# Attention and a gated feed-forward layer on one core: one load moves up the queue, three visits move by part of a step

## The chip, the core and the metric

The kernel runs on one core of a Trainium2 chip. A core has TensorE (PE in the rows: matmuls, with weight loads beside them as PEld), VectorE (DVE), ScalarE (ACT), GpSimd (POOL) and SyncE (SP), which here only issues DMAs. They run side by side and wait for each other through semaphores. SBUF is the working memory, PSUM the memory that TensorE writes; DMAs move data between device memory and SBUF. The metric is the device time of one launch in microseconds (us).

## The reference

Eight batches of attention with eight heads of 64, 576 positions, a window of 128 keys and a linear bias, and behind it a feed-forward layer over all 4608 rows: 512 to 2048, an activation, 2048 to 512.

```python
scores = scale * np.matmul(q, k.transpose(0, 1, 3, 2))
mask = (rel >= 0) & (rel < window)
scores = np.where(mask, scores + bias[None], -1000000000.0)
scores = scores - np.max(scores, axis=-1, keepdims=True)
attn = np.exp(scores)
attn = attn / (np.sum(attn, axis=-1, keepdims=True) + 1e-09)
x = np.matmul(attn, v)            # heads side by side: 4608 rows of 512
h = x @ w_in
sp = np.where(h > 20.0, h, np.log1p(np.exp(np.minimum(h, 20.0))))
g = h * np.tanh(sp)
out = g @ w_out
```

## The kernel before

**The work.** The feed-forward layer runs in nine blocks: block c holds the first 512 rows of batch c (c from 0 to 7), and the ninth the last 64 rows of all batches, which were put aside in `xs`. A block has two layers. The first layer makes `h` (names `h`) in 8 pieces from x and the weights `si`; the activation turns it into `g`. The second layer takes 32 steps: each is 6 matmuls of 128x512 into one of two sums `po0`, `po1`, from the weights `so` and from a high and a low part of g, `gg`. ScalarE makes the high part by a copy, GpSimd the low part by a subtraction. After step 15 both sums are copied out as `ob`, and step 16 starts the next sums in the same PSUM banks. Every float32 product is made of three matmuls in a rounded form.

Attention of batch c+1 is laid between the matmuls of block c, in four pairs of heads. The first two batches are written out by hand in one list of names, `FIRST_STEPS` (line 28): there TensorE, VectorE, ScalarE, GpSimd and SyncE keep the list's order. From block 1 on, attention of batch c+1 (c from 1 to 6, six blocks) is placed by a table of numbers, and there only TensorE and SyncE keep the program's order; a scheduler orders the rest.

**The corners.** The last 64 queries of a pair of heads are laid out in the corners of a 128x128 square, so that one matmul scores two heads. For the second batch (batch 1) all four squares come by one load, `load_corners(1)`, into the tile `z1` (rows: `z`, 256 KB). That tile takes the one buffer of tag `pta`, which held the values of the last pair of batch 0 (`v0_3`); the matmuls `lV3`, which write `pt_3l`, read those last. `lC3` copies that pair's last small result and sends it to `xs` by SyncE. Before the change the load of the corners is issued behind the last piece of block 0's first layer (`Q7`): there the last weights (`wo7`, two halves), two loads of values (`v1_0`, `v1_1`) and then the corners go out on SyncE's queue. The first user of z1 is `lbS0`, the last-query scores of batch 1's first pair, in the middle of the first steps of block 0's second layer. Behind it in TensorE's order stand the scores `bS0` and `bS1` and then the next steps of the second layer.

While block 0 runs, the weights are still being turned into their rounded forms (`cE`, `cW`, `cU`, `cL` in the list, on ScalarE, VectorE, ScalarE and GpSimd; `wo`, `to`, `so` in the rows).

**The visits.** In blocks 1 to 6 the steps of the second layer have the keys 0 to 31, and the making of `gg` for step pair m the key 2m - 4.1. Attention is put in by the same kind of key, through the four numbers of `VISITS`. Visit k is where pair k's weights meet the values: `rest_values`, `values`, `keep`, `split_x`. The scores of pair p+2 stand just ahead of visit p (their own number is 0.001 less), and the softmax of that pair follows at fractions of the way to the next visit: biases and row minima on VectorE (they write the tile `pz`), exponentials on ScalarE, the scaling on GpSimd, a transposition in squares on VectorE, and the way out to device memory by SyncE (`d<-pz`; a first group of 384 KB, a second of 320 and 96 KB). Between `pz` in SBUF and the values stands a way back in: `pta<-d` and `ptb<-d`, issued behind the visit before. SyncE issues per visit: four `pta` and two `ptb` loads, the next pair of q and k (`qk`), the small result (`xs<-xo`), at one visit a load of values (`v`), then the three `d<-pz`.

`pz` has two buffers. So the first bias of pair 3 (ahead of visit 1) waits until the first `d<-pz` of pair 2 has left its buffer. The exponentials of pair 3 stand on ScalarE ahead of the two copies `ob` that step 16 waits for.

```python
        VISITS = (5.0, 13.3, 21.6, 29.9)
        def when(x):
            k = min(max(int(x // 1), 0), 2)
            return VISITS[k] + (VISITS[k + 1] - VISITS[k]) * (x - k)
```

With these numbers the scores of pair 2 get the key 4.99, ahead of step 5, and the values of pair 0 get 5.0 and a little more, behind step 5: step 5 stands between them. The other visits have all their parts between the same two steps.

Of the kernel before, what the change touches and what calls it, by code (L numbers as in the profile page):

```python
# [80 lines left out]
def attention_mish_mlp(  # L81
# [83 lines left out]
    def load(dst, src):  # L165
        sp.dma_start(out=dst, in_=src)

    def load_w(kind, j):

        n = 256 if kind == "i" else DM  # L170
        if kind == "i":
            src = w_in[:, j * 256 : (j + 1) * 256].rearrange("(c p) f -> p c f", p=P)
        else:
            src = w_out[j * 256 : (j + 1) * 256, :].rearrange("(c p) f -> p c f", p=P)
        if (kind, j) == last_w:

            halves = [
                xp.tile([P, 1024], U32, tag=f"x{NCC - 2 + a}", name=f"w{kind}{j}_{a}")
                for a in range(2)
            ]  # L180
        else:
            t = big(f"w{kind}{j}", U32)
            halves = [t[:, :1024], t[:, 1024:]]
        raw_w[(kind, j)] = halves
        for a, t in enumerate(halves):
            part = src[:, a * (512 // n) : (a + 1) * (512 // n), :]
            if bits:
                load(t.rearrange("p (c n) -> p c n", n=2 * n), part.bitcast(U32))
            else:
                load(t[:, :512].bitcast(F32).rearrange("p (c n) -> p c n", n=n), part)  # L190
# [77 lines left out]
    def parts_of(t):  # L268

        qk = t[:, : 2 * S].rearrange("p (a s) -> p a s", a=2)  # L270
        return lambda h, n0, n: qk[h, 0, n0 : n0 + n], lambda h, n0, n: qk[h, 1, n0 : n0 + n]
# [35 lines left out]
    def load_pair(b, p):  # L307
        t = at.tile([P, 2 * S], F32, tag="qk", name=f"qk{b}_{p}")
        load(t, qk_[b, p][:, : 2 * S])
        qkv[(b, p)] = parts_of(t)  # L310

    def load_v(b, p):

        pl, tag = (at, "pta") if (b, p) == (0, NP - 1) else (xp, f"x{p}")
        t = pl.tile([P, 2, 4, P], F32, tag=tag, name=f"v{b}_{p}", bufs=1)
        load(t, v[b, p])
        qkv[("v", b, p)] = ((t[:, 0], t[:, 1]), t[:64, 1, 3])
# [3 lines left out]
    def load_corners(b):  # L321

        t = corners[b] = at.tile([P, 2, 4, P], F32, tag="pta", name=f"z{b}", bufs=1)
        load(t[:, 0], qk_[b, :, :, 2 * S :].rearrange("a p n -> p a n"))
# [652 lines left out]

    def attention(b):

        VISITS = (5.0, 13.3, 21.6, 29.9)  # L980

        def when(x):
            k = min(max(int(x // 1), 0), 2)
            return VISITS[k] + (VISITS[k + 1] - VISITS[k]) * (x - k)

        def next_pair(p):
            nxt = (b, p + 2) if p + 2 < NP else (b + 1, p + 2 - NP)
            if nxt[0] < B:
                load_pair(*nxt)

        ahead, steps = {}, []
        for p in range(NP):
            if p > 1:
                steps += pair_steps(b, p) + [(p - 1.993, lambda p=p: next_pair(p))]
                continue
            before, beside, behind, in_out, ends = pair_steps(b, p)

            ahead[4 + 2 * p] = (before + [lambda p=p: next_pair(p)], beside, behind)
            if p:
                steps.append((0.005, in_out))  # L1000
            else:
                ahead[5] = ([], [], [in_out])
            steps += ends
        steps = [(when(x), f) for x, f in steps]

        steps += [(d, lambda p=p: load_v(b, p)) for p, d in enumerate((-0.5, -0.4, 6.5, 17.5))]
        return ahead, sorted(steps, key=lambda s: s[0])
# [152 lines left out]

    loads = {f"bS{2 * p + 1}": lambda p=p: load_pair(*((1, p + 2) if p < 2 else (2, p - 2))) for p in range(NP)}
    loads.update({f"bL{p}": lambda p=p: load_v(1, p + 2) for p in range(2)})
    loads.update({f"L{p + 2}": lambda p=p: load_pair(1, p) for p in range(2)})

    def add_conversions(ms):
        for m in ms:
            tag = f"po{m % 2}" if m < 6 else "wo"[m % 2]
            works = convert(*conv[m], tag, m in BY_ACT, dve if m == len(conv) - 1 else pool)
            steps.update(zip((f"cE{m}", f"cW{m}", f"cU{m}", f"cL{m}"), works))

    add_conversions(range(len(conv) - 2))
    for name in FIRST_STEPS.split():
        steps[name]()
        if name in loads:
            loads[name]()
        if name == f"Q{NJ - 1}":
            load_w(*last_w)
            add_conversions(range(len(conv) - 2, len(conv)))
            for p in range(2):
                load_v(1, p)  # L1180
            load_corners(1)
    dve.fixed = act.fixed = pool.fixed = False

    for c in range(1, B + 1):
        ahead, steps_beside = attention(c + 1) if c + 1 < B else ({}, [])
        for j in range(NJ):
            before, beside, behind = ahead.get(j, ([], [], []))
# [115 lines left out]
```

## Time and profile before

| | us |
|---|---|
| median of three runs | 951.16 |
| lowest and highest | 950.44, 953.33 |
| the profiled execution | 953.0 |
| its span, first to last instruction | 951.2 |
| TensorE busy in it | 931.4 |

The span is the time from the first to the last instruction of one profiled execution; launch and end lie around it. TensorE is busy in 98% of it, so what can be won is what TensorE waits for, and what it does more slowly than it does the same thing elsewhere. The timeline merges instructions of one kind that follow each other: a row gives start, length, engine, what is written and read, and how many; in square brackets stand the idle time before it and who ended it. Rows of matmuls overlap their successors by a little, since the ends of matmuls are modelled: the distance of two starts is the time that a group takes.

### The profile page before, as it was taken

What the parts mean: (1) busy time and instruction counts of PE and PEld (TensorE: products, weight loads), DVE (VectorE), ACT (ScalarE), POOL (GpSimd) and SP (SyncE); (2) the same over time, 40 slices, a digit from 0 to 9 for tenths busy, and PEclk for the clock granted to TensorE, in tenths of its full rate; (3) what the DMA queues carried; (4) which work ended last, traced back from release to release, by engine and by line L of the source; (5) the groups of instructions that cost most, each with busy time, mean ns of one, the idle gap of its engine ahead of it and who ended that gap; (6) DMA issues with size and microseconds to landing.
All of it is one profiled execution on the core that took longest, in us unless ns stands there. A gap on an engine that the chain in (4) does not pass through costs nothing.

```text
span 951.2 us, 17253 instructions
## 1 busy us (share of the span) xinstructions
PE 931.4 (98%) x6650; PEld 759.8 (80%) x6650; DVE 284.6 (30%) x1119; ACT 434.5 (46%) x1075; POOL 332.0 (35%) x300
## 2 busy tenths in 40 slices
PE   8997999999999999999999999999999999999998
PEld 6785888888888788887888788887888888888886
DVE  5996861333122510423033411341043300100000
ACT  6996752654254613744256424552374422322221
POOL 4585752135122531244123512244124411241042
PEclk9998999999999999999999999999999999999999
DMA  9963120337215540556024720545044520000001
GB/s 345 393 254 119 66 88 24 98 125 233 62 42 158 156 141 23 154 157 183 24 77 131 224 86 26 173 125 171 24 127 137 164 63 1 23 22 23 1 20 25
DMA packets 89745, 106.63 MB, mean 112 GB/s; under 512 B 22720, under 2 KB 69824, under 8 KB 89664
## 3 DMA queue, kind: packets, MB, share of 16 engines
q1 hardware_dynamic: 89664, 105.54, 34.7%
q8 instruction: 52, 0.85, 0.4%
q14 instruction: 29, 0.24, 0.1%
HBM read 75.37 MB, written 30.15 MB: 111 GB/s over the span
## 4 chain that ended last, share of the span: by engine, by line
PE 89%; ACT 5%; DMA 3%; DVE 1%; issue 1%; POOL 1%; SPq 0%; DVEq 0%; ACTq 0%; POOLq 0%
PE h L69 40%; PE po L69 38%; PE s L69 3%; PE o L69 3%; ACT pz L69 3%; DMA d<-pz 1%; PE w L69 1%; PE po0s L69 1%; PE os L69 1%; DMA v<-in_v_dram 1%; DMA z<-in_qk_dram 1%; DVE pz L69 1%; SPq L69 0%; ACT x L69 0%; POOL pz L69 0%
## 5 line engine op out<-in xcount | busy, mean ns | idle before, releaser
L69 PE MATMUL po<-so,gg 128*128 128x512 f32 x1728 | 407.7, 393 | 5.1 <-ACT ob L69 5.1
L69 PE MATMUL h<-x,si 128*128 128x512 f32 x1728 | 398.2, 390 | 0.0
L69 PEld LDWEIGHTS po<-so,gg 128*128 128x128 f32 x1728 | 321.2, 188 | 77.6 <-ACT ob L69 7.6
L69 PEld LDWEIGHTS h<-x,si 128*128 128x128 f32 x1728 | 323.0, 188 | 70.3 <-issue 3.3
L69 POOL TENSOR_TENSOR gg<-g,gg 128x512 fp32r<-128x512 f32 x144 | 185.2, 1288 | 412.1 <-ACT gg L69 411.8
L69 ACT ACTIVATE gg<-g 128x512 fp32r<-128x512 f32 x144 | 90.7, 630 | 177.6 <-PE po L69 175.3
L69 ACT ACTIVATE g<-h 128x1024 f32<-128x1024 f32 x72 | 73.9, 1027 | 193.5 <-PE h L69 193.4
L69 POOL TENSOR_TENSOR pz<-pz,sm 128x256 f32<-128x256 f32 (+4 forms) x96 | 97.2, 1030 | 168.1 <-DVE sm L69 141.2
L69 ACT ACTIVATE pz<-pz,mx 128x192 f32<-128x192 f32 (+1 forms) x280 | 120.2, 431 | 19.8 <-DVE mx L69 19.2
L69 DVE CUSTOM_DVE_ANT_0 pz<-s,nb 128x192 f32<-128x192 f32 (+1 forms) x160 | 46.9, 328 | 107.6 <-PE s L69 84.5
L69 ACT ACT_TABLE_LOAD x39 | 50.0, 1283 | 13.9 <-DVE mx L69 13.4
L69 DVE STREAM_TRANSPOSE pz<-pz 128x768 f32<-128x768 f32 (+2 forms) x72 | 49.2, 709 | 17.8 <-POOL pz L69 16.8
L69 DVE CUSTOM_DVE_ANT_0 pz<-os,nb 128x192 f32<-128x192 f32 x24 | 8.5, 355 | 151.5 <-PE ws L69 151.5
L69 ACT ACTIVATION_READ_ACCUMULATOR pz<-pz,mx 128x1 f32 x280 | 52.3, 187 | 0.0
L69 DVE COPY ob<-po 128x512 f32<-128x512 f32 x10 | 6.9, 692 | 137.4 <-PE po L69 137.4
L69 DVE COPY xo<-w 128x64 f32<-128x64 f32 x24 | 5.4, 224 | 116.1 <-PE w L69 115.7
L69 ACT ACTIVATE x<-o 128x256 fp32r<-128x256 f32 (+1 forms) x32 | 12.8, 401 | 46.6 <-PE w L69 46.1
L69 PEld LDWEIGHTS o<-pta,v 64*64 64x64 f32 (+1 forms) x768 | 27.7, 136 | 8.1 <-issue 6.4
L69 PE MATMUL o<-pta,v 64*64 64x64 f32 (+1 forms) x768 | 32.8, 226 | 0.0
L69 ACT ACTIVATE ob<-po 128x512 f32<-128x512 f32 x26 | 14.8, 593 | 34.1 <-PE po L69 34.1
L69 DVE DVE_READ_ACCUMULATOR2_ANT mx<- 128x1 f32 (+1 forms) x360 | 29.0, 81 | 0.0
L69 PE MATMUL s<-qk 64*64 64x192 f32 (+1 forms) x560 | 28.0, 326 | 0.0
(188 smaller groups left out, 579.1 us busy)
## 6 DMA issues: line engine op xcount, KB each, us to landing
v<-in_v_dram SPq DMA_DIRECT2D x32, 512.0 KB, 4.7
qk<-in_qk_dram SPq DMA_DIRECT2D x28, 576.0 KB, 4.6
d<-pz SPq DMA_DIRECT2D x24, 384.0 KB, 2.8
pta<-d SPq DMA_DIRECT2D x72, 128.0 KB, 2.8
wi<-in_moe_w_in_dram SPq DMA_DIRECT2D x16, 512.0 KB, 11.0
wo<-in_moe_w_out_dram SPq DMA_DIRECT2D x16, 512.0 KB, 10.2
out_dram<-ob SPq DMA_DIRECT2D x32, 256.0 KB, 2.0
d<-pz SPq DMA_DIRECT2D x24, 320.0 KB, 4.0
```

Of the source, the lines that this page charges most:

```text
L69: ins = method(*args, **kwargs)
```

## The change

The load of batch 1's corners is taken from behind `Q7` and put behind `lC3`, the copy of batch 0's last small result. `VISITS` becomes (5.5, 13.5, 21.5, 29.9).

```diff
-        VISITS = (5.0, 13.3, 21.6, 29.9)
+        VISITS = (5.5, 13.5, 21.5, 29.9)
...
     loads.update({f"bL{p}": lambda p=p: load_v(1, p + 2) for p in range(2)})
+    loads["lC3"] = lambda: load_corners(1)
     loads.update({f"L{p + 2}": lambda p=p: load_pair(1, p) for p in range(2)})
...
             for p in range(2):
                 load_v(1, p)
-            load_corners(1)
```

No instruction is added or removed. SyncE's queue at the end of block 0's first layer, before the change (`xs_95<-xo0_3l` is the last small result, `z1` the corners, `wo7` the last weights, `v1` values of batch 1):

```order
L69 DMA qk1_1_677<-in_qk_dram 128x1152
L69 DMA xs_95<-xo0_3l_734 128x64
L69 DMA wo7_0_1049<-in_moe_w_out_dram 128x1024
L69 DMA wo7_1_1050<-in_moe_w_out_dram 128x1024
L69 DMA v1_0_1054<-in_v_dram 128x1024
L69 DMA v1_1_1056<-in_v_dram 128x1024
L69 DMA z1_1058<-in_qk_dram 128x4x128
```

There the corners are the last of the seven. The same place on SyncE after the change:

```order
L69 DMA qk1_1_677<-in_qk_dram 128x1152
L69 DMA xs_95<-xo0_3l_734 128x64
L69 DMA z1_737<-in_qk_dram 128x4x128
L69 DMA wo7_0_1051<-in_moe_w_out_dram 128x1024
L69 DMA wo7_1_1052<-in_moe_w_out_dram 128x1024
L69 DMA v1_0_1056<-in_v_dram 128x1024
L69 DMA v1_1_1058<-in_v_dram 128x1024
```

The corners now stand ahead of four loads that they stood behind; all else on this queue keeps its place, here and in the rest of the program.

TensorE at visit 0 of block 1, before the change (`po1_0_1<-so2` is step 5, `s2_2` the scores of pair 2, `o2_0` and `w2_0` the first of the values of pair 0):

```order
L69 MATMUL po1_0_0_2218<-so2_181,gg1_0_2_2215 128x512 x6
L69 MATMUL s2_2_0_2256<-qk2_2_1997 64x192 x8
L69 MATMUL s2_2_1_2268<-qk2_2_1997 64x128 x4
L69 MATMUL s2_2_1_2268<-qk2_2_1997 64x192 x6
L69 MATMUL po1_0_1_2225<-so2_181,gg1_0_2_2215 128x512 x6
L69 MATMUL o2_0_2288<-pta2_0_2077,v2_0_2211 64x64
```

Step 5 stands between scores and values. The same place on TensorE after the change:

```order
L69 MATMUL po1_0_0_2218<-so2_181,gg1_0_2_2215 128x512 x6
L69 MATMUL po1_0_1_2225<-so2_181,gg1_0_2_2215 128x512 x6
L69 MATMUL s2_2_0_2262<-qk2_2_1997 64x192 x8
L69 MATMUL s2_2_1_2274<-qk2_2_1997 64x128 x4
L69 MATMUL s2_2_1_2274<-qk2_2_1997 64x192 x6
L69 MATMUL o2_0_2288<-pta2_0_2077,v2_0_2211 64x64
```

Step 5 moved from between the scores and the values to ahead of both. The same six times, in blocks 1 to 6; TensorE's order is otherwise unchanged, also at the other three visits.

VectorE behind the biases of pair 2 in block 1, before the change (`sm` are the sums of the softmax, `pz2_2_0` and `pz2_2_1` the two groups of pair 2, `xo2_0` and `x2_0` results of pair 0):

```order
L69 RECIPROCAL sm2_2_0_2266<-sm2_2_0_2266 128x4
L69 RECIPROCAL sm2_2_1_2280<-sm2_2_1_2280 128x5
L69 STREAM_TRANSPOSE pz2_2_0_2267<-pz2_2_0_2267 128x768
L69 COPY xo2_0_2330<-w2_0_2289 128x64
L69 TENSOR_TENSOR x2_0_2333<-o2_0_2288,x2_0_2333 128x256
L69 TENSOR_TENSOR x2_0_2333<-w2_0_2289,x2_0_2333 128x2x128
L69 STREAM_TRANSPOSE pz2_2_1_2281<-pz2_2_1_2281 128x640
L69 STREAM_TRANSPOSE pz2_2_1_2281<-pz2_2_1_2281 128x2x96
```

The first transposition stands third. The same place on VectorE after the change:

```order
L69 RECIPROCAL sm2_2_0_2272<-sm2_2_0_2272 128x4
L69 COPY xo2_0_2330<-w2_0_2289 128x64
L69 TENSOR_TENSOR x2_0_2333<-o2_0_2288,x2_0_2333 128x256
L69 RECIPROCAL sm2_2_1_2286<-sm2_2_1_2286 128x5
L69 TENSOR_TENSOR x2_0_2333<-w2_0_2289,x2_0_2333 128x2x128
L69 STREAM_TRANSPOSE pz2_2_0_2273<-pz2_2_0_2273 128x768
L69 STREAM_TRANSPOSE pz2_2_1_2287<-pz2_2_1_2287 128x640
L69 STREAM_TRANSPOSE pz2_2_1_2287<-pz2_2_1_2287 128x2x96
```

The copy and the two subtractions for pair 0 now stand ahead of the first transposition. On ScalarE the copy `gg` for steps 10 and 11 moved from between pair 2's exponentials to ahead of them, and one copy of pair 0's result to ahead of the second group's sums; on GpSimd the low part of the same `gg` moved to ahead of pair 2's first scaling. At visit 1 none of the engines' orders changes.

## Rows read from the trace of the kernel before

**Rows 1.** The page: busy us of each engine and its share of the span

```profile
PE 931.4 (98%) x6650; PEld 759.8 (80%) x6650; DVE 284.6 (30%) x1119; ACT 434.5 (46%) x1075; POOL 332.0 (35%) x300
```

**Rows 2.** Waits of TensorE in the span: for whom, us in total, times, longest

```profile
PE s L69 <- DMA z<-in_qk_dram: 6.0, 1, 6.0
PE po L69 <- ACT ob L69: 5.1, 6, 1.4
```

**Rows 3.** Timeline of TensorE in block 0: start, us, instructions, [idle before]

```profile
41.23 0.60 PE L69 MATMUL pt_3l<-pf_3l,v 128*64 128x64 f32 x8
...
88.90 0.91 PE L69 MATMUL s<-qk,z 128*64 128x96 f32 x8 [6.02 <-DMA z<-in_qk_dram]
89.74 2.63 PE L69 MATMUL s<-qk 64*64 64x128 f32 x32
92.29 11.76 PE L69 MATMUL po<-so,gg 128*128 128x512 f32 x48
103.89 1.04 PE L69 MATMUL s<-ident,pz 128*128 128x128 f32 x8
...
107.74 0.55 PE L69 MATMUL s<-qk,z 128*64 128x96 f32 x8
...
109.80 1.42 PE L69 MATMUL s<-qk 64*64 64x128 f32 x32
```

**Rows 4.** Stretches: length, busy PE PEld DVE ACT POOL, clock, DMA share, GB/s

```profile
82.88:88.90 6.02, 0.00 (x0) 0.03 (x1) 0.87 (x2) 3.13 (x4) 4.73 (x4) 0.82 0.74 267
88.90:92.30 3.40, 3.40 (x41) 2.34 (x41) 0.64 (x4) 0.47 (x3) 0.00 (x0) 0.50 0.03 5
```

**Rows 5.** Timeline of SyncE's issues, end of block 0's first layer, and block 1

```profile
60.16 0.33 SPq L69 DMA_DIRECT2D xs<-xo_3l  x1
79.55 1.01 SPq L69 DMA_DIRECT2D wo<-in_moe_w_out_dram  x2
...
215.24 2.15 SPq L69 DMA_DIRECT2D d<-pz  x3
```

**Rows 6.** The chain of waits in order of time, one piece

```profile
81.55 7.21 DMA z<-in_qk_dram
```

**Rows 7.** Timeline of ScalarE and GpSimd behind the wait in block 0

```profile
91.83 0.45 ACT L69 ACTIVATE pz<-pz,mx 128x192 f32<-128x192 f32 x1 [5.39 <-DVE mx L69]
...
95.93 0.63 ACT L69 ACTIVATE gg<-g 128x512 fp32r<-128x512 f32 x1 [1.11 <-PE po L69]
...
99.56 2.04 POOL L69 TENSOR_TENSOR pz<-pz,sm 128x512 f32<-128x512 f32 x2
```

**Rows 8.** Timeline of TensorE in block 1, visits 0 and 1

```profile
205.04 1.75 PE L69 MATMUL s<-qk 64*64 64x192 f32 x36
206.72 1.66 PE L69 MATMUL po<-so,gg 128*128 128x512 f32 x6
...
210.11 11.18 PE L69 MATMUL po<-so,gg 128*128 128x512 f32 x48
221.21 1.57 PE L69 MATMUL s<-qk 64*64 64x192 f32 x33
...
224.52 3.04 PE L69 MATMUL po<-so,gg 128*128 128x512 f32 x12
227.78 8.46 PE L69 MATMUL po<-so,gg 128*128 128x512 f32 x36 [0.22 <-ACT ob L69]
```

**Rows 9.** Timeline of VectorE in block 1, pair 2 and the first bias of pair 3

```profile
212.67 0.94 DVE L69 STREAM_TRANSPOSE pz<-pz 128x768 f32<-128x768 f32 x1
...
222.16 0.36 DVE L69 CUSTOM_DVE_ANT_0 pz<-s,nb 128x192 f32<-128x192 f32 x1 [6.20 <-PE s L69]
```

**Rows 10.** DMA issues: count, KB, median us to landing; whole span, then 213.5 to 217

```profile
d<-pz SPq DMA_DIRECT2D x24, 384.0 KB, 2.8
...
v<-in_v_dram SPq DMA_DIRECT2D x1, 512.0 KB, 5.9
d<-pz SPq DMA_DIRECT2D x1, 384.0 KB, 6.4
```

## The prediction, made before the changed kernel ran

> **What bounds the kernel now.** I read the page first: TensorE is busy for 931.4 of 951.2 us [rows 1], so 19.8 us of idle time is all that waiting costs, and a change of order can win little more. Next the waits of TensorE: one wait of 6.0 us for the corners z, the largest of all, and six of together 5.1 us, at most 1.4, for the copies ob [rows 2]. These six are one a block, in blocks 1 to 6, at step 16. Then the timeline around both places, because a wait has two sides: what came late, and what would have come late next.
>
> In block 0 the reader is to see three things. TensorE stops at 82.88 (88.90 less 6.02) and starts again at 88.90 [rows 3]; the corners, issued at 81.55, took 7.21 us [rows 6] and land at 88.76, so nothing else held it. And TensorE is slow afterwards: the granted clock is 0.50, the lower of its two levels (1.2 GHz), from 88.90 to 92.30, while it was 0.82 as a mean of the idle stretch [rows 4]. A mean of 0.82 between 1.00 and 0.50 says that the clock fell 64% into the stretch, some 3.9 us after TensorE stopped.
>
> In the six blocks TensorE loses time without any wait: at visit 0 one step of the second layer stands between scores and values. From the scores' start to the next full run of steps go 210.11 - 205.04 = 5.07 us; at visit 1 scores and values in one piece take 224.52 - 221.21 = 3.31 us, and a step in a run of eight takes (221.21 - 210.11) / 8 = 1.39 us [rows 8].
>
> **Part 1, the corners.** The load moves from behind the last weights (79.55) to behind the last small result (60.16) [rows 5]. Its buffer is free by then: the last reader of v0_3 is done at 41.83 [rows 3]. I put its issue within 2 us of 60.16; even with the 7.2 us that it took before it lands by 70, 13 us ahead of 82.88. It is moved past four loads on SyncE's queue, none of which is issued before 79.55, so nobody waits behind it. It adds no wait. What falls away:
>
> - the wait: 6.02 us [rows 3];
> - the slow restart. Last-query scores, 8 matmuls: 0.91 against 0.55 later, 0.36. Scores, 32 matmuls: 2.63 against 1.42, 1.21 [rows 3]. First 48 matmuls of the second layer: 11.76 against 11.18 for 48 in block 1, 0.58 [rows 3, 8]. Together 2.15.
>
> That is 8.17 us. What is late next? ScalarE sat idle for 5.39 us ahead of its first exponential and 1.11 us more ahead of its next gg [rows 7]: what stands on it ahead of the exponentials keeps its time, so its stream moves up by only 5.4 to 6.5 us and falls 1.7 to 2.8 us behind TensorE. The nearest place where that is felt is the transpositions at 103.89 [rows 3], which read what GpSimd finishes at 101.60 [rows 7]: 2.29 us of cover. At 1.7 this costs nothing, at 2.8 it costs 0.5. I take nothing, since ScalarE's second gap closes too, and keep 0.5 for the range. The clock: without the pause I expect 1.00 throughout. A gain here beyond 8.17 has no source, as the stretch behind it has no further wait.
>
> **Part 2, the visits.** Step 5 moves ahead of the scores. Visit 0 then is made of a step and one piece, 1.39 + 3.31 = 4.70 instead of 5.07: 0.37 us less, six times, 2.2 us. It could be less if the first step behind a piece is slower than its run's mean; six steps and the visit in one piece, by rows of visit 1, bound it at 0.3. The range of this part is 1.9 to 2.2; I take 2.2. The other three visits change their numbers but not their place between the same two steps.
>
> The cost to look for is in the softmax of pair 2. Its scores start 1.39 us later, and the order on VectorE puts the copy and two subtractions for pair 0 ahead of the first transposition, which wait for ScalarE. The transposition of the first group started 212.67 - 205.04 = 7.63 us after the scores' start and ended at 8.57 [rows 8, 9]. I add 1.39 and about 0.4 for the two subtractions (an estimate: they and the second reciprocal come after ScalarE's copies): ended at 10.4. SyncE's turn for this group's d<-pz came at 215.24, 10.20 after the same point [rows 5]; its row of issues begins when the values of pair 0 end, which is 0.37 earlier, so at 9.83. So the issue slips by 0.55 us against its turn.
>
> Does that reach TensorE? The first bias of pair 3 waits for this DMA to land, the exponentials for the bias, ob for the exponentials, step 16 for ob. In block 1 the bias starts at 222.16, 0.95 after the scores [rows 8, 9], and the DMA lands at 215.24 + 6.4 = 221.7 [rows 5, 10]: some 0.5 to spare, and the wait at step 16 is 0.22 [rows 8]. Since six waits make 5.1 with the longest 1.4 [rows 2], in some blocks the landing must be late already: by 5.1 - 6 x 0.22 = 3.8 us in all and at most 1.4 - 0.22 = 1.2 in one, which takes four blocks. There a later landing goes into the wait one for one. But what sets the landing? The load of values issued 0.53 us ahead lands at 214.71 + 5.9 = 220.6, and d<-pz 1.1 us behind it, although it takes 2.8 us from issue to landing in the median of all 24 [rows 10]. So it stands in a queue of transfers, and an issue as late as 221.7 - 2.8 = 218.9 would land at the same time. The slip of 0.55 is within that; and the loads ahead go out 0.37 us earlier, as visit 1 does. I cost it at nothing. The other bound, landing 0.55 later in every block, is 4 x 0.55 where it is late already and nearly nothing in the other two: 2.2 us.
>
> The Trainium skill (DMA: Bandwidth & Descriptors, queues, rings and completion order) says that descriptors of one issuing engine's queue are consumed in ring order on each DMA engine. The landing of d<-pz 1.1 us behind a load that went out ahead of it agrees with that. By this rule the landing follows the loads ahead and the time is the forecast; if each transfer instead took its own 6.4 us from issue, the bound of 2.2 us would be paid.
>
> **The sum.** 8.17 + 2.2 = 10.4 us. Against the profiled execution: 953.0 - 10.4 = 942.6 (span 951.2 to 940.8). That execution is 1.84 us above the median of the three runs, and a run of the kernel varies by such an amount; against the median 951.16 the sum gives 940.8.
>
> **The rivals.**
>
> 1. *The weights' conversion becomes the bound in block 0.* For it: ScalarE, VectorE and GpSimd still make rounded weights there, and the wait gave them time: in it GpSimd was busy for 4.73 and ScalarE for 3.13 of 6.02 us [rows 4]. Against it: 2.29 us of cover at the nearest place. If TensorE stops for the whole lag of 2.8 us: 943.6.
> 2. *The split costs nothing.* If the 0.37 us is only how the ends of matmuls are modelled, part 2 gives 0: 943.0. Against it: the 5.07 and 3.31 are distances of starts.
> 3. *The landing moves with the transposition, and step 16 pays.* If d<-pz lands later by all that the transposition slips against visit 1, 1.8 + 0.37 = 2.15 us, four late blocks pay 2.15 and the other two 2.15 less the 0.5 to spare: 8.6 + 3.3 = 11.9, so 952.7: no change. Against it: SyncE's turn comes after the transposition today.
> 4. *The same, and the clock falls: slower.* The place is step 16 of the late blocks. Their waits would be up to 1.4 + 2.15 = 3.55 us, close to the 3.9 us after which the clock fell in block 0. If it falls in four blocks, each pays the restart of 2.15 us again: 952.7 + 8.6 = 961.3. It decides from a landing that is some 2.2 us later than now (13.3 us lost over six blocks, the 10.4 won and 2.9 more). Against it: the longest of these waits is 1.4 today. The Trainium skill (TensorE: Matmul & The Clock Gate, HAM oscillation) warns that waits for data in a loop can send the array back to the half clock each time; block 0 shows one such fall, and no row here shows one at step 16.
> 5. *The waits at step 16 shrink.* If the loads ahead of d<-pz meet less traffic because they go out earlier against it, up to the 3.8 us of lateness go: 937.0. For it: block 1, with the same program, waits only 0.22. Against it: the 0.37 is won on both sides of that race, by the loads and by visit 1.
>
> **How the numbers follow.** Forecast 0.66, with its own range 939.5 to 942.5; rival 1 0.08, rival 2 0.10, rival 3 with its small forms (the 2.2 us, 943.0) 0.08, rival 4 0.02, rival 5 0.06. The range takes in the forecast, rivals 1 and 2, and the small form of rival 3: 938.8 to 944.5. A measurement of this kernel tells 0.3%, 2.9 us, from no change. All but rivals 3 and 4 are faster by more than that: faster 0.93, same 0.05, slower 0.02.
>
> **What would show it.** In the profile of the changed kernel: no wait for z; the 32 scores of batch 1's first pair at 1.4 us with the clock at 1.00; scores and values at visit 0 in one piece of 3.3 us; the six waits for ob at 5.1 us in all, give or take one. It would be wrong if TensorE waits for GpSimd or ScalarE between the scores and the transpositions of block 0 (rival 1), if the step at visit 0 is not shorter (rival 2), or if the waits for ob grow beyond 7 us and the first bias of pair 3 names d<-pz in most blocks (rival 3).

## The result and the profile after

| | before | changed |
|---|---|---|
| median, first comparison | 951.58 | 942.88 |
| median, second comparison | 952.63 | 941.56 |
| the profiled execution | 953.0 | 942.93 |
| its span | 951.2 | 941.1 |

The ratio of the first comparison is 0.9906 (95%: 0.9889 to 0.9924), 8.7 us between the medians; that of the second, with the same changed kernel, 0.9885 (0.9871 to 0.9898), 11.1 us. The forecast was 10.4, to 940.8 us. The profiled executions differ by 10.1.

The page and the waits of TensorE (for whom, us in total, times, longest) of the changed kernel answer to [rows 1] and [rows 2]:

```profile
PE 928.6 (99%) x6650; PEld 760.8 (81%) x6650; DVE 285.0 (30%) x1119; ACT 434.0 (46%) x1075; POOL 332.1 (35%) x300
```

```profile
PE po L69 <- ACT ob L69: 3.8, 6, 1.4
...
PE s L69 <- DVE mx_1l L69: 1.0, 1, 1.0
```

The wait for z is gone, that for ob is 3.8 instead of 5.1, and a new one has come: 1.0 us for `mx_1l`, the bias of pair 1's last queries on VectorE. The timeline of TensorE in block 0, as [rows 3]:

```profile
80.59 2.88 PE L69 MATMUL po<-so,gg 128*128 128x512 f32 x12
83.40 0.55 PE L69 MATMUL s<-qk,z 128*64 128x96 f32 x8
83.88 1.42 PE L69 MATMUL s<-qk 64*64 64x128 f32 x32
85.24 11.18 PE L69 MATMUL po<-so,gg 128*128 128x512 f32 x48
96.25 1.03 PE L69 MATMUL s<-ident,pz 128*128 128x128 f32 x8
...
103.32 1.42 PE L69 MATMUL s<-qk 64*64 64x128 f32 x32 [1.02 <-DVE mx_1l L69]
```

The scores take 0.55 and 1.42 where they took 0.91 and 2.63. The first steps, ahead of these rows in the kernel before:

```profile
80.00 2.88 PE L69 MATMUL po<-so,gg 128*128 128x512 f32 x12
```

From the first steps to the transpositions go 96.25 - 80.59 = 15.66 us against 103.89 - 80.00 = 23.89 [rows 3]: 8.23 won. The granted clock (third number from the end) over the two stretches of [rows 4] is 1.00, and in SyncE's timeline the corners are issued at 59.61, ahead of the last weights [rows 5]:

```profile
82.88:88.90 6.02, 6.02 (x59) 4.62 (x58) 5.41 (x26) 5.20 (x11) 5.25 (x5) 1.00 0.94 348
88.90:92.30 3.40, 3.40 (x17) 2.81 (x16) 3.02 (x6) 3.34 (x14) 1.76 (x3) 1.00 0.05 22
```

```profile
59.61 0.38 SPq L69 DMA_DIRECT2D z<-in_qk_dram  x1
80.14 1.01 SPq L69 DMA_DIRECT2D wo<-in_moe_w_out_dram  x2
```

TensorE in block 1, as [rows 8]:

```profile
199.94 1.57 PE L69 MATMUL s<-qk 64*64 64x192 f32 x33
...
203.24 11.20 PE L69 MATMUL po<-so,gg 128*128 128x512 f32 x48
...
214.37 1.57 PE L69 MATMUL s<-qk 64*64 64x192 f32 x33
...
220.93 8.45 PE L69 MATMUL po<-so,gg 128*128 128x512 f32 x36 [0.22 <-ACT ob L69]
```

Visit 0 now reads like visit 1: 203.24 - 199.94 = 3.30 us in one piece.

The account of the two profiled executions: 8.23 in block 0, less 1.16 that the new wait takes back (from transpositions to the scores behind it 103.32 - 96.25 = 7.07 against 109.80 - 103.89 = 5.91), 6 x 0.37 = 2.2 at the visits, 1.3 at step 16, less 0.59 by which the second layer's steps began later (80.59 against 80.00, with the same program up to there): 10.0 of 10.1.

### The profile page after: what moved, and what is told of

Read it like the earlier page. It is cut to its first block, busy times and chain, and to the rows that moved or that the text cites. A ratio compares the mean times of both kernels' runs of the same rounds, so it can differ in the third digit from the quotient of the medians.

```text
span 941.1 us, 17254 instructions
## 1 busy us (share of the span) xinstructions
PE 928.6 (99%) x6650; PEld 760.8 (81%) x6650; DVE 285.0 (30%) x1119; ACT 434.0 (46%) x1075; POOL 332.1 (35%) x300
## 4 chain that ended last, share of the span: by engine, by line
PE 87%; ACT 6%; DVE 2%; DMA 2%; issue 1%; POOL 1%; SPq 0%; DVEq 0%; ACTq 0%; POOLq 0%
PE h L69 41%; PE po L69 37%; ACT pz L69 3%; PE s L69 3%; PE o L69 3%; DMA d<-pz 1%; PE w L69 1%; DVE pz L69 1%; PE po0s L69 1%; PE os L69 1%; ACT x L69 1%; DMA first<-in_qkb_dram 0%; ACT to L69 0%; ACT so L69 0%; POOL pz L69 0%
```

## The experiments

Ratios are against the kernel before, run beside each on the same chip.

| kernel | median | ratio (95%) | waits for ob | other wait in block 0 |
|---|---|---|---|---|
| corners alone | 945.14 | 0.9919 (0.9907, 0.9932) | 4.2 | mx_1l 1.0 |
| visits alone | 948.82 | 0.9961 (0.9948, 0.9973) | 3.4 | z 5.5 |
| bias ahead | 940.81 | 0.9876 (0.9861, 0.9891) | 6.7 | |
| values behind | 940.43 | 0.9870 (0.9857, 0.9883) | 1.3 | mx_1l 1.0 |
| changed, again | 941.56 | 0.9885 (0.9871, 0.9898) | 5.2 | mx_1l 1.0 |
| both edits | 939.37 | 0.9857 (0.9842, 0.9872) | 1.3 | |
| values behind, split | 942.29 | 0.9889 (0.9875, 0.9902) | 1.3 | mx_1l 1.0 |
| corners half way | 948.04 | 0.9948 (0.9936, 0.9961) | 4.4 | z 3.0 |
| stop filled, 44 | 952.61 | 1.0001 (0.9993, 1.0009) | 2.3 | mx_1l 0.5 |
| stop filled, 24 | 951.36 | 0.9992 (0.9978, 1.0006) | 3.3 | z 2.4 |
| visit 0 at 4.5 | 939.86 | 0.9873 (0.9858, 0.9888) | 1.3 | mx_1l 1.0 |
| visit 0 at 6.5 | 952.12 | 0.9984 (0.9968, 1.0001) | 10.0 | mx_1l 1.0 |

The first four ran on one chip, the next four on a second and the last four on a third; the last two columns are sums in us from each profiled execution.

**Each part alone.** From the changed kernel:

```diff
-        VISITS = (5.5, 13.5, 21.5, 29.9)
+        VISITS = (5.0, 13.3, 21.6, 29.9)
```

> The corners' load alone is moved; the visits keep the numbers of before. If the two parts are independent and each is worth what its own stretch shows: the wait for z (6.0) and the slow restart (2.15) go, a wait of some 1.0 us for the bias of pair 1's last queries on VectorE comes, so 8.2 - 1.1 = 7.1 us less than before, 944.3 us, with the six waits for ob still at 5.1 us in all. If the visits give nothing (rival 2): the whole gain of both parts, 942.9 us.

From the kernel before:

```diff
-        VISITS = (5.0, 13.3, 21.6, 29.9)
+        VISITS = (5.5, 13.5, 21.5, 29.9)
```

> The visits alone are moved; the corners' load stays where it was. If the whole step at visit 0 is worth 0.37 us six times: 949.2 us; if the waits for ob shrink with it, as in the changed kernel (5.1 to 3.8), 947.9 us. If the split costs nothing (rival 2): 951.4 us, no change. The wait of 6.0 us for z and the clock of 0.50 behind it are still there in every case.

The corners give 0.81%, 7.7 us (6.5 to 8.9 by the interval), against 7.1 expected; the visits 0.39%, 3.7 us (2.6 to 5.0). The two ratios multiply to 0.9880. The whole change measures 0.9885 in the second comparison and 0.9906 in the first, so the parts add up to the whole as well as two comparisons of the whole agree, and no better. The visits alone gave more than the 2.2 us of their six steps, and the interval leaves 2.2 out. What the rest is stays open. It is no steady fall of the waits for ob: the five profiled kernels with the old first number show 5.1, 4.2, 4.4, 2.3 and 3.3, the four with 5.5 and nothing else at the visits 3.8, 5.2, 6.7 and 3.4. One and the same program shows 3.8 and 5.2.

**Where the new wait comes from.** In the hand-written list, on top of the changed kernel:

```diff
-bX1 bX0 cW31 cW30 U50 lbX0 R7 bM0 U51 lbS1 cL29 bM1 bV0 R6 lbM0 cU30 lbV0 cU31 cL31 lbT1 lbE1 lbA1
+bX1 bX0 cW31 cW30 U50 lbX0 R7 bM0 U51 lbS1 cL29 bM1 bV0 R6 lbM0 cU30 lbV0 lbT1 cU31 cL31 lbE1 lbA1
```

`lbT1` is that bias; `cU31` and `cL31` are the cast and the subtraction of the last conversion, which VectorE does itself.

> The changed kernel with VectorE's order turned around at one place: the bias of pair 1's last queries stands ahead of the last weight conversion (a cast and a subtraction, 1.13 + 1.65 us), not behind. If VectorE's order is what the new wait of 1.0 us in block 0 comes from, it goes: 941.9 us, and the weights converted 0.4 us later are missed by nobody. If block 0 is held by something else that is as late (the copies of weights on ScalarE, GpSimd's low parts), a wait of about the same length appears behind it: 942.9 us.

The wait is gone from TensorE's list, and 0.47 us for GpSimd shows at a later transposition. That is half a microsecond net; the 2 us between this median and the first of the changed kernel come from two comparisons and say no more. The mechanism stands in the timelines of GpSimd and VectorE: before, after, and with the bias ahead:

```profile
106.19 1.31 POOL L69 TENSOR_TENSOR so<-wo,so 128x512 fp32r<-128x512 f32 x1 [0.78 <-ACT so L69]
...
107.37 0.42 DVE L69 CAST so<-wo 128x512 fp32r<-128x512 f32 x1
...
109.39 0.34 DVE L69 CUSTOM_DVE_ANT_0 pz_1l<-s,nl 128x192 f32<-128x192 f32 x1
```

```profile
99.72 1.30 POOL L69 TENSOR_TENSOR so<-wo,so 128x512 fp32r<-128x512 f32 x1 [0.79 <-ACT so L69]
...
100.18 1.13 DVE L69 CAST so<-wo 128x512 fp32r<-128x512 f32 x1
...
102.91 0.34 DVE L69 CUSTOM_DVE_ANT_0 pz_1l<-s,nl 128x192 f32<-128x192 f32 x1
```

```profile
100.86 1.29 POOL L69 TENSOR_TENSOR gg<-g,gg 128x512 fp32r<-128x512 f32 x1
...
100.67 0.36 DVE L69 CUSTOM_DVE_ANT_0 pz_1l<-s,nl 128x192 f32<-128x192 f32 x1 [0.50 <-PE s L69]
100.96 1.50 DVE L69 CAST so<-wo 128x512 fp32r<-128x512 f32 x1
```

Before, the bias ended just as TensorE needed its bank at 109.80: there was no cover. TensorE moved up by 103.89 - 96.25 = 7.64 us, the bias by 109.39 - 102.91 = 6.48. Of the 1.16 between them 0.45 was lost ahead of the cast (107.37 - 100.18 = 7.19), where VectorE had waited 0.61 us for TensorE's transpositions before and didn't wait after, and 0.71 in the cast: it took 0.42 us before and 1.13 after. In all three timelines it ends 0.29 to 0.31 us after the GpSimd instruction that runs at its start (107.79 and 107.50, 101.31 and 101.02, 102.46 and 102.15), and in all fourteen profiled executions 0.27 to 0.31 us after it, whether it took 0.42 or 1.52. So it waits for it. The Trainium skill (SBUF — State Buffer, SBUF: two separate sides) describes such a lock: for some kinds of VectorE instruction, VectorE and GpSimd share a pair of ports, and whichever instruction starts first keeps it to its end. These three rows agree; no row says which kind the cast is.

**What step 16 waits for.** Pair 2's values load behind the stores of its weights:

```diff
-        steps += [(d, lambda p=p: load_v(b, p)) for p, d in enumerate((-0.5, -0.4, 6.5, 17.5))]
+        steps += [(d, lambda p=p: load_v(b, p)) for p, d in enumerate((-0.5, -0.4, 9.6, 17.5))]
```

> The changed kernel with the load of the third pair's values (512 KB) issued behind the three stores of pair 2's weights and not ahead of them. If the first store's landing is set by what stands ahead of it in the queue: it lands some 1.0 to 1.4 us earlier against visit 1, the bias of pair 3 that waits for it starts as much earlier where it is late, and the six waits for ob fall from 3.8 us to near 6 x 0.22 = 1.3 us: 940.4 us. If a store takes its own 6.3 us from issue whatever stands ahead: no change, 942.9 us. If the values then land too late for their visit, TensorE waits for v: slower than 943.

It came out as the queue has it: 1.3 us in all, six times 0.22. In block 2 the first bias of pair 3 (timeline of VectorE, changed kernel and this one) no longer names the store:

```profile
318.30 0.36 DVE L69 CUSTOM_DVE_ANT_0 pz<-s,nb 128x192 f32<-128x192 f32 x1 [5.24 <-DMA d<-pz]
```

```profile
316.57 0.36 DVE L69 CUSTOM_DVE_ANT_0 pz<-s,nb 128x192 f32<-128x192 f32 x1 [4.81 <-PE s L69]
```

In block 3 of the changed kernel, where step 16 waited for 1.22 us, the first bias is on time. There the fifth one, which opens the second group, waits for a store:

```profile
423.91 0.36 DVE L69 CUSTOM_DVE_ANT_0 pz<-s,nb 128x192 f32<-128x192 f32 x1 [1.14 <-DMA d<-pz]
```

With the values behind, the stores don't go out earlier: in block 3 the first is issued at 414.99 in the changed kernel and at 412.54 here, 8.80 us after the start of pair 2's scores in both (406.19 and 403.74). They land sooner. The first two stores of that block (KB, us from issue to landing), in the changed kernel and then here:

```profile
d<-pz SPq DMA_DIRECT2D x1, 384.0 KB, 6.2
d<-pz SPq DMA_DIRECT2D x1, 320.0 KB, 7.0
```

```profile
d<-pz SPq DMA_DIRECT2D x1, 384.0 KB, 4.9
d<-pz SPq DMA_DIRECT2D x1, 320.0 KB, 5.3
```

From the other side came two kernels with another first number, the second with the values' number moved along so that SyncE's order stays:

```diff
-        VISITS = (5.5, 13.5, 21.5, 29.9)
+        VISITS = (4.5, 13.5, 21.5, 29.9)
```

```diff
-        VISITS = (5.5, 13.5, 21.5, 29.9)
+        VISITS = (6.5, 13.5, 21.5, 29.9)
...
-        steps += [(d, lambda p=p: load_v(b, p)) for p, d in enumerate((-0.5, -0.4, 6.5, 17.5))]
+        steps += [(d, lambda p=p: load_v(b, p)) for p, d in enumerate((-0.5, -0.4, 7.5, 17.5))]
```

> The changed kernel with the first number of the visits at 4.5 instead of 5.5: visit 0 is again in one piece, but ahead of step 5 and not behind it, so all that goes out behind visit 0 on SyncE's queue (loads of pair 1's weights, q and k, values, the stores of pair 2's weights) starts 1.39 us earlier against step 16. If the landing of the first store, which stands behind these loads, is what step 16 waits for: the six waits go from 4 to 5 us down to near 1.3, as with the values behind the stores: 939 us, against 942 for the changed kernel. If the stores' landing does not matter: no change. If ScalarE's copies gg for steps 10 and 11, which now stand behind the exponentials, come too late: TensorE waits for them in six blocks, slower than the changed kernel.

> The changed kernel with the first number of the visits at 6.5 instead of 5.5, and the load of pair 2's values moved along by as much (7.5), so that SyncE's order is the same: visit 0 is in one piece, a step later, and all that goes out behind it on SyncE's queue is 1.39 us later against step 16. If step 16 waits for the landing of the first store, as the kernel with 4.5 says from the other side: the six waits grow by 1.39 us where they are late already and by somewhat less where they are on time, from 4 to 5 us to some 11 to 13 in all, 949 us; and since a stop of 3.0 us was enough in block 0 to bring the clock down, the longest of them, at 3 us, may cost a slow stretch besides, up to 953 us. If the landing doesn't follow the visit: no change, 942 us.

At 4.5 the six waits are again 1.3 us and the time is 939.86. At 6.5 they are 10.0, and the kernel loses nearly all that the change had won. Its twelve runs lie between 947.1 and 954.9 us; the two below 949 have a mean granted clock of 0.997 and 0.999, the two above 954 one of 0.993 and 0.994. The timeline of TensorE at step 16, blocks 1, 4 and 5, and then the granted clock of the first 3 us in blocks 1 and 4:

```profile
221.64 10.07 PE L69 MATMUL po<-so,gg 128*128 128x512 f32 x36 [1.99 <-ACT ob L69]
...
537.04 8.46 PE L69 MATMUL po<-so,gg 128*128 128x512 f32 x36 [2.03 <-ACT ob L69]
...
641.99 9.93 PE L69 MATMUL po<-so,gg 128*128 128x512 f32 x36 [2.60 <-ACT ob L69]
```

```profile
221.64:224.64 3.00, 3.00 (x7) 2.32 (x8) 1.96 (x3) 0.95 (x2) 2.79 (x3) 0.53 0.85 270
537.04:540.04 3.00, 3.00 (x13) 2.50 (x14) 2.01 (x3) 0.95 (x2) 2.85 (x3) 1.00 0.94 264
```

In blocks 1, 2 and 5 the clock fell to the lower level behind waits of 1.99, 1.81 and 2.60 us, and the next 36 matmuls took up to 1.6 us more than 8.46; in block 4 a wait of 2.03 cost nothing beyond itself. Against the second profiled execution of the changed kernel (span 941.3): 10.0 - 5.2 = 4.8 for the waits and 1.6, 1.6 and 1.5 for the clock make 9.5 of the 9.6 by which the span, 950.9, is longer. This is rival 4, one step of the visit away. The Trainium skill (TensorE: Matmul & The Clock Gate, HAM oscillation) tells of waits in a loop that send the array back to the half clock. This trace agrees, three times in six blocks, behind shorter waits than those of the Trainium skill's example.

**The split by itself.** With the values behind the stores the waits for ob are at 0.22 each; there the first number goes back.

```diff
-        VISITS = (5.5, 13.5, 21.5, 29.9)
+        VISITS = (5.0, 13.5, 21.5, 29.9)
```

> The kernel with the values of pair 2 behind the stores, and the first number of the visits back at 5.0, so that step 5 again stands between scores and values at visit 0; the other visits as changed. There the waits for ob are down to 0.22 each, so the split is measured by itself. If a split costs what the distances of starts show: 0.37 six times, 2.2 us more than with the values behind and no split, 942.6 us, with the waits for ob still at 1.3 us. If it is only how matmuls' ends are modelled (rival 2): 940.4 us.

Beside it ran the changed kernel once more, with no edit:

> The changed kernel itself once more, as the measure for the kernels run beside it. Same program as before: a ratio of 0.9906 within its interval. If the waits for ob in the six blocks are set anew in each execution by what the DMA queues happen to carry, the profiled execution shows another sum than 3.8 us for them (between 1.3 and 7), and its time differs from the other's by that and by the start (0 to 1.3 us).

Step 16 of blocks 1 and 6, with the split and then without:

```profile
220.91 8.45 PE L69 MATMUL po<-so,gg 128*128 128x512 f32 x36 [0.22 <-ACT ob L69]
...
735.58 8.45 PE L69 MATMUL po<-so,gg 128*128 128x512 f32 x36 [0.22 <-ACT ob L69]
```

```profile
219.63 8.45 PE L69 MATMUL po<-so,gg 128*128 128x512 f32 x36 [0.22 <-ACT ob L69]
...
732.40 8.45 PE L69 MATMUL po<-so,gg 128*128 128x512 f32 x36 [0.22 <-ACT ob L69]
```

Five blocks take 514.67 and 512.77 us: 0.38 a block. The ratios differ by 0.19%, 1.8 us, with intervals that overlap, so it is the starts that decide: the split costs what they said.

**The slow restart by itself.** Corners half way, from the kernel before:

```diff
+            load_corners(1)
             for p in range(2):
                 load_v(1, p)
-            load_corners(1)
```

> The kernel before with the corners ahead of the two loads of values and still behind the last weights: no other change, the visits as before. They are issued at 80.6 and should land at about 85.5, a little behind the last weights (84.61 before). TensorE then stops at 82.9 for some 2.6 us, not 6.0. If only a stop longer than the 3.9 us after which the clock fell costs a restart: the clock stays at 1.00, and 3.4 of the wait and all 2.15 of the restart go, 5.6 us less than before, less a few tenths for a small wait on VectorE behind it: 946 to 947 us. If any stop costs the restart: 3.4 less, 948 to 949 us.

Its timeline of TensorE, and then the clock of two stretches:

```profile
85.28 0.55 PE L69 MATMUL s<-qk,z 128*64 128x96 f32 x8 [3.00 <-DMA z<-in_qk_dram]
85.77 2.40 PE L69 MATMUL s<-qk 64*64 64x128 f32 x32
88.10 11.82 PE L69 MATMUL po<-so,gg 128*128 128x512 f32 x48
99.76 1.04 PE L69 MATMUL s<-ident,pz 128*128 128x128 f32 x8
```

```profile
85.28:86.00 0.72, 0.72 (x16) 0.60 (x20) 0.00 (x0) 0.57 (x1) 0.72 (x2) 1.00 0.99 404
86.00:88.10 2.10, 2.10 (x33) 1.34 (x25) 0.65 (x4) 0.49 (x3) 1.04 (x1) 0.51 0.27 105
```

The expectation that a stop shorter than 3.9 us leaves the clock alone fell: TensorE stood for 3.00 us, worked again for 0.7 at the full clock, and only then did it fall. From these scores to the transpositions go 14.48 us; before it was 103.89 - 88.90 = 14.99 [rows 3], after it is 96.25 - 83.40 = 12.85. So a stop of 3.00 costs a restart of 1.63, that of 6.02 one of 2.14: any stop of these costs a restart, the second reading of the two. The price doesn't follow the length: in the kernel with the visits alone a stop of 5.49 was followed by 104.72 - 89.09 = 15.63 us over the same stretch, a restart of 2.78. The time of the kernel half way fell by 0.52%, 4.9 us (3.7 to 6.1). That takes in 5.6 and leaves out 3.4, so by itself it would have spoken for the wrong reading. The two profiled executions show why: 3.02 less of waiting and 0.51 less of restart make 3.5, and 0.6 came from an earlier start of these steps (79.40) and 0.7 from the waits for ob.

In the two kernels with a filled stop, TensorE multiplies the identity by itself, into the bank that the scores then write over (44 times, or 24).

```diff
+            for _ in range(44 if p == 0 else 0):
+                pe.matmul(t[:, 0, :P], lhsT=ident, rhs=ident, start=True, stop=True, skip_group_check=True)
```

> The kernel before, with 44 more matmuls of 128x128 (the identity by itself, 0.13 us each, 5.8 us in all) ahead of the first scores that read the corners, into the bank that these scores then write over: TensorE works through the stop for z instead of standing still, and nothing else is changed. They wait for nothing, the corners land when they did, so the wait that is left is about 0.2 us. If the 2.15 us behind the stop are the clock, and the clock falls because TensorE stands still: it stays at 1.00, the scores take 0.55 and 1.42, and the time is 2.15 less than before, 950.6 us against some 952.7, while ScalarE's lag behind costs nothing. If the slow stretch has another cause (the landing weights and values, PSUM, the conversion): no change, 952.7 us.

> As the kernel with 44 more matmuls ahead of the scores that read the corners, but 24, since each proved to be two records of 0.113 us: 5.4 us of work in the stop for z. TensorE then reaches these scores some 0.3 us behind or ahead of the corners' landing. If the clock is all that the slow stretch was: from the start of the second layer's steps to the transpositions 23.89 - 2.15 + 0.3 = 22.0 us, and about 2 us less than before as a whole, a wait for VectorE behind it of up to 0.5 taken off again: 950.5 to 951 us, ratio 0.9985. If part of the slow stretch stays: no change.

```profile
81.72 9.98 PE L69 MATMUL s<-ident 128*128 128x128 f32 x88
91.64 0.55 PE L69 MATMUL s<-qk,z 128*64 128x96 f32 x8
92.12 1.43 PE L69 MATMUL s<-qk 64*64 64x128 f32 x32
93.47 11.20 PE L69 MATMUL po<-so,gg 128*128 128x512 f32 x48
104.51 1.03 PE L69 MATMUL s<-ident,pz 128*128 128x128 f32 x8
```

The first rows are those with 44. The filling was sized wrongly: each gave two records, 9.98 us in all, so the corners' scores started 12.64 us after the first steps (91.64 - 79.00) and not 8.90. What matters is behind them: at the full clock 104.51 - 91.64 = 12.87 us to the transpositions, as in the changed kernel, though the weights and values land and the conversion runs as before. The 2.14 is the clock, and the clock falls because TensorE stands. The time as a whole didn't follow: 3.74 of filling less 2.12, and 0.62 lost at the bias behind it (111.04 - 104.51 = 6.53 against 5.91), should be 2.2 slower, and the ratio is 1.0001. In the profiled executions an earlier start of the steps (1.0) and smaller waits for ob (2.3 instead of 5.1) more than make up for it; why these waits are smaller there isn't settled. With 24 the corners landed late, at 90.1; a wait of 2.38 was left and the slow stretch came again. That run is inconclusive on the time, and one more case of a short stop (the corners' scores and the transpositions):

```profile
90.16 0.55 PE L69 MATMUL s<-qk,z 128*64 128x96 f32 x8 [2.38 <-DMA z<-in_qk_dram]
...
104.61 1.04 PE L69 MATMUL s<-ident,pz 128*128 128x128 f32 x8
```

14.45 us, 1.60 over the full clock's 12.85.

**Both edits on top of the change,** those of the bias and of the values:

> The changed kernel with both edits: the bias of pair 1's last queries ahead of VectorE's last conversion, and the values of pair 2 behind the stores of pair 2's weights. If the two waits are independent: against the changed kernel 3.8 - 1.3 = 2.5 less at step 16 and 1.0 less 0.5 (the wait for GpSimd that showed instead) in block 0, 3.0 us in all, 939.9 us. If block 0 gives nothing in the end: 940.4 us.

Against the changed kernel beside it the median falls by 2.2 us, 939.37 against 941.56, and the intervals touch only at their ends. It has the lowest median of this study, but its interval overlaps with those of the kernel with the values behind and of the kernel with 4.5 for 5.5, which each change one number of the changed kernel.

## Why the prediction was right, and where not

**Part 1** was right in its two terms: the wait of 6.02 went, and the restart measured 2.14 for 2.15; 8.23 to the transpositions for 8.17. The step that failed is "What is late next?". It named the transpositions as the nearest place and found 2.29 us of cover there; that held, since they started without a wait. But it followed ScalarE and GpSimd, not VectorE, and stopped at the first place. One place on, the scores of pair 1 need the bank that the last-query bias reads, and in the trace of before that bias ended (109.73) as TensorE needed it (109.80): hardly any cover. VectorE moved up 1.16 us less than TensorE, and 1.16 was paid. "A gain beyond 8.17 has no source" was right; "I take nothing" and the 0.5 kept for the range were too small.

**Part 2** was right: 0.38 a block by the kernel with the split, 0.37 forecast. The store's issue was forecast at 10.4 us against the old place of the scores; the first transposition started at 207.70, 7.76 behind the scores, so 9.15 by the old place, and ended at 10.1. That costs nothing that can be seen: 3.8 and 5.2 us for ob in two executions of the changed kernel, against 5.1. The reason was right too, since taking the 512 KB ahead of the store away took the lateness away. The chain was drawn too narrowly: it had only the first bias of pair 3 wait for the first store, and in block 3 the fifth bias and a later store set step 16. The forecast that the waits stay "give or take one" was too narrow for what one program shows in two executions.

**The rivals.** Rival 1 came in a small form, on another engine and at another place: 1.16 instead of 2.8 us. Rival 2 fell. Rival 3 didn't occur, but its price is real: one step later at visit 0 costs 4.8 us of waits. Rival 4 was underrated in its threshold: it was set at waits of 3.55 us, and falls came behind 1.81, 1.99, 2.38 and 2.60, though not behind every such wait. The longest wait of the changed kernel is 1.4 in one profiled execution and 1.8 in the other, nearer to that edge than the prediction knew. Rival 5's 3.8 us of lateness were there to be had, by other edits: with the values behind the stores, or with 4.5, six times 0.22 is all that is left.

**The sum.** 10.4 was forecast. The account gives 8.23 + 2.2 less 1.16, or 9.3, and scatter of the start and of step 16 can make 8.7 and 11.1 of it between medians. The missed 1.16 is smaller than that scatter, which is why the number held. That the profiled executions differ by 10.1, so near to 10.4, is luck: 1.3 at step 16, which was not forecast and doesn't come each time, made up for the 1.16.

## What to carry to other kernels

When a wait on the path goes, follow every engine that had its pause too, VectorE as well as the ones that look busiest, over several places: the cover that counts is between a producer's end and its consumer's start in the old trace, place by place, and an engine that keeps its own pace uses it up. A load that nobody needs for 10 us should not stand in a queue ahead of a store that somebody waits for; look at what goes out just ahead of the late transfer before moving work on the engines. Price a wait on TensorE as its length and a chance of a slow restart of 1.5 to 2.8 us: of eight stops of 1.81 to 3.00 us five were followed by one here, and both of 5.5 and 6.0 were.

## What the runs showed of the hardware that was not expected

- The clock fell after stops of 2.38 and 3.00 us in block 0, and of 1.81, 1.99 and 2.60 at step 16, but not after 2.03 there, nor after 1.82 and 2.05 at step 16 of the kernel with the bias ahead. In four of these five falls TensorE was already working again, for 0.2 to 0.9 us. So the stop's length alone doesn't decide, and what else does is open.
- A cast of 128x512 on VectorE took 0.42 to 1.52 us, by how much of a GpSimd instruction was left when it began.
- The start scatters. The same 32 scores of the first pair in the first 9 us, in the changed kernel and in that with the values behind:

```profile
6.24 2.62 PE L69 MATMUL s<-first 64*64 64x192 f32 x32 [0.63 <-DMA first<-in_qkb_dram]
```

```profile
6.14 1.46 PE L69 MATMUL s<-first 64*64 64x192 f32 x32 [0.46 <-DMA first<-in_qkb_dram]
```

The program is the same up to there, yet the second layer's first steps then start at 80.59 and 79.34. One execution does the same work at little more than half the pace, as block 0's scores did at the lower clock (2.63 for 1.42), but the profile gives a granted clock of 1.00 for both; whether the clock is the cause is not shown. This may be part of why medians of one kernel lie up to 1.4 us apart.
